# Two of six groups of a first matrix product in a second pass, five of eight blocks with seven products for eight

## The chip, the cores and the metric

The kernel runs on one core of a Trainium2 chip. The metric is device time in microseconds: the time of one execution, as a median over several runs. A profile of one execution is read beside it; its times are counted from the first instruction of its span.

The engines are named as in the profile: PE is TensorE (matrix products), PEld its loading of weights, DVE is VectorE, ACT is ScalarE, POOL is GpSimd, and SP is the engine that only issues DMAs here. Each engine takes its instructions in order.

## The reference

A block of linear attention with decay feeds a mixer. Everything is float32.

```python
# attention: batch 4, 8 heads, 768 positions, head size 64; blocks of 64 positions
intra = ((qb @ kb.T) * Dmask) @ vb
out[block] = intra + (qb * lam_pow) @ kv_state
kv_state = lam_block * kv_state + (kb * rev_pow).T @ vb

# mixer on x = attention output as (4, 768, 512)
h = x.transpose(0, 2, 1) @ U @ V           # U: 768 x 32, V: 32 x 768
u = x + h.transpose(0, 2, 1)
ch = np.maximum(u @ w_ch1, 0.0) @ w_ch2    # w_ch1: 512 x 2048, w_ch2: 2048 x 512
return u + ch
```

The two products with w_ch1 and w_ch2 are the bulk: 3,072 rows of u, 512 columns, 2,048 columns of the hidden layer.

## The kernel before

**Numbers.** The weights and the vectors arrive as 64-bit words; VectorE and ScalarE turn them into float32 on the chip. A conversion of one tile (128 x 512) has five VectorE steps (L166, L155, L184, L192, L197) and two ScalarE steps between them that make the exponents (L173, L174); the tiles `sc` and `m` that it works in exist once. A float32 factor is then split into a high part, a low part and a third, and a product of two factors takes three matrix products in a reduced format: high x high and low x low parts that go into a bank `pz`, and third x third into a bank `pd`; the result is `(4096 + 1) * pz + 4096 * pd`. This is why each 128 x 128 tile of weights costs three instructions of 512 columns.

**Stages.** (1) Attention over 24 tiles of 128 positions, up to about 114 us. Every tile's result `x_nat` gets the low-rank mix added (L571 for the last batch), is transposed on TensorE (L604 for the last eight tiles) and split into `u_hl` and `u_d`, and is stored to memory as `u_d` for the end. (2) The first product: u has six groups `g` of 512 positions, w_ch1 has 16 tiles `ft` of 128 hidden columns. `hidden(ft, pair)` does two groups for one `ft`: 16 matrix products into two `pz`, 8 into two `pd`, a ScalarE scaling (L844), a VectorE sum (L853) and a store of r to memory. (3) The second product: for each group and each `ft`, r is fetched, made positive and split (L952 on ScalarE, L953 and L954 on VectorE), and multiplied with w_ch2's tile, 12 matrix products; at the end of a group u is added (L994, and L998 on GpSimd) and the result goes out.

**Order.** Up to the end of the first six units of the first product (`head`), every engine's order is written out by hand (`manual_schedule`). There the last eight tiles of attention are mixed and transposed between the products (`rest`, `at`), and the conversions stand as `side` steps after given units. Afterwards a scheduler orders the instructions. `body` is the loop over `ft` with three pairs each, with the conversion and splitting of w_ch1's next tile (`w1_steps`) and of w_ch2 (`w2_steps`) as side steps; `tail` runs the last three `ft` pair by pair, so that the groups' places `hl` and `d` come free for w_ch2, which `w2_back` loads from memory, already split.

**Banks.** Eight banks, four tags (a1, a2, b1, b2) of two. A unit takes two for `pz` and two for `pd`, and units alternate between a and b.

Of the kernel before, what the change touches and what calls it, by code (L numbers as in the profile page):

```python
# [18 lines left out]
def kernel(  # L19
# [61 lines left out]
    mix_ctx = ctx.enter_context(ExitStack())  # L81
    att_ctx = ctx.enter_context(ExitStack())
# [19 lines left out]
    w2_d = [dram.tile([P, 3, C], FP32, name=f"w2_d{ft}") for ft in range(FT)]  # L102
# [100 lines left out]
    def split_steps(tile_of, src, in_parts=False, scale=None, apart=False):  # L203

        st = {}

        def dst():
            if "w" not in st:
                st["w"] = wconv.tile([P, C], FP32, tag="wf", name="wf")
            return st["w"]  # L210

        def five():
            st["o"] = o = tile_of()
            st["t"] = o[:, 0, :].bitcast(FP32)
            on_scalar(lambda: nc.scalar.mul(o[:, 0, :], st["w"], NEAR))  # L215

        def six():
            w, low = st["w"], st["o"][:, 1, :]
            st["low"] = low.bitcast(FP32) if scale is None else w
            nc.vector.tensor_tensor(  # L220
                out=low if scale is None else w, in0=w, in1=st["t"], op=ALU.subtract
            )
            if scale is not None:
                on_scalar(lambda: nc.scalar.mul(low, w, scale))

        def seven():
            nc.vector.scalar_tensor_tensor(
                st["o"][:, 2, :], st["t"], -E, st["low"], ALU.mult, ALU.add
            )

        return weight_steps(dst, src, C, in_parts=in_parts, apart=apart) + [five, six, seven]

    w1v, w2v = {}, {}

    def w1_steps(ft, in_parts=False, apart=False):
        def tile_of():
            w1v[ft] = w1_pool.tile([P, 3, C], F32R, tag="w1", name="w1")
            return w1v[ft]

        cols = moe_w_ch1[:, ft * P : (ft + 1) * P].rearrange("(c p) f -> p c f", p=P)  # L240
        return split_steps(tile_of, cols, in_parts, apart=apart)
# [340 lines left out]
    def columns(what, g, ct):  # L582
        return what[:, ct, :] if g >= FG else by_halves(what)[:, :, ct, :]

    def like(out, g):
        return out if g >= FG else out.rearrange("p (t i) -> p t i", i=D)

    hl_at, d_at = [hl_pool], [d_pool]
# [4 lines left out]
    def turn(s):  # L593

        g, n = divmod(s, TG)
        if n == 0:
            uhl[g] = hl_at[g >= FG].tile([P, 2, CT, N], F32R, tag="hl", name="u_hl")
            ud[g] = d_at[g >= FG].tile([P, CT, N], F32R, tag="d", name="u_d")
        if g >= FG:
            cols = slice(n * P, (n + 1) * P)  # L600
            hi, low, diff = uhl[g][:, 0, :, cols], uhl[g][:, 1, :, cols], ud[g][:, :, cols]
            pt = bank([P, CT, P], "put", "b1")
            for ct in range(CT):
                nc.tensor.transpose(  # L604
                    out=pt[:, ct, :], in_=xs[s][:, ct * P : (ct + 1) * P], identity=ident
                )
            store(s)
            del xs[s]
            nc.scalar.mul(hi, pt, E * NEAR)
            nc.vector.scalar_tensor_tensor(  # L610
                low, hi.bitcast(FP32), -1.0 / E, pt, ALU.mult, ALU.add
            )
            nc.gpsimd.tensor_tensor(
                out=diff, in0=hi.bitcast(FP32), in1=low.bitcast(FP32), op=ALU.subtract
            )
            return
# [187 lines left out]
    def enter_first_product(s):  # L804
        nonlocal r_pool
        att_ctx.close()
        words_pool[:] = [wconv]
        for pools, name in ((hl_at, "hl_b"), (d_at, "d_b")):
            pools.append(
                ctx.enter_context(tc.tile_pool(name=name, bufs=NG - FG, reuse_waits="tile"))  # L810
            )
        r_pool = ctx.enter_context(tc.tile_pool(name="r", bufs=4, reuse_waits="tile"))
        set_ends(r_pool.tile([P, 2], FP32, tag="ends", bufs=1, name="ends"))
# [9 lines left out]
    def hidden(ft, pair, before={}):  # L823
# [9 lines left out]
        for ct in range(CT):  # L833
            for n in range(2):
                for g in pair:
                    others()
                    nc.tensor.matmul(  # L837
                        out=like(acc[g][0], g), lhsT=w[:, n, ct, :],
                        rhs=columns(uhl[g][:, n], g, ct),
                        start=(ct == 0 and n == 0), stop=(ct == CT - 1 and n == 1),  # L840
                    )
# [3 lines left out]
        for ct in range(CT):  # L845
            for g in pair:
                others()
                nc.tensor.matmul(  # L848
                    out=like(acc[g][1], g), lhsT=w[:, 2, ct, :], rhs=columns(ud[g], g, ct),
                    start=(ct == 0), stop=(ct == CT - 1),  # L850
                )
# [4 lines left out]
    def w2_steps(ft):  # L856
        def tile_of():
            w2v[ft] = w2_pool.tile([P, 3, C], F32R, tag="w2", name="w2")
            return w2v[ft]

        def keep():
            nc.sync.dma_start(out=w2_d[ft], in_=w2v.pop(ft).bitcast(FP32))

        rows = moe_w_ch2[ft * P : (ft + 1) * P, :]
        return split_steps(tile_of, rows, scale=4096.0) + [keep]


    w2hl, w2dd = {}, {}

    def w2_back(ft):  # L870
        n, i = divmod(ft, 4)
        if i == 0:
            w2hl[n] = hl_pool.tile([P, 4, 2, C], F32R, tag="hl", name="w2_hl")
            w2dd[n] = d_pool.tile([P, 4, C], F32R, tag="d", name="w2_d")
        nc.sync.dma_start(out=w2hl[n][:, i].bitcast(FP32), in_=w2_d[ft][:, 0:2, :])
        nc.sync.dma_start(out=w2dd[n][:, i].bitcast(FP32), in_=w2_d[ft][:, 2, :])

    pairs = [(g, g + 1) for g in range(0, NG, 2)]

    LAST = FT - 3  # L880
    body = [(pair, ft) for ft in range(2, LAST) for pair in pairs]
    tail = [(pair, ft) for pair in pairs for ft in range(LAST, FT)]

    def run_units(units, side, every=lambda i: None):
        for i, (pair, ft) in enumerate(units):
            hidden(ft, pair)
            for step in side[len(side) * i // len(units) : len(side) * (i + 1) // len(units)]:
                step()
            every(i)

# [15 lines left out]
    head = [(pair, ft) for two in (pairs[:2], pairs[2:]) for ft in (0, 1) for pair in two]  # L906
    side = list(zip((0,), last[4:])) + list(zip((0, 3, 3, 3, 4, 4, 4, 4), w1_steps(2)))
    for i, (pair, ft) in enumerate(head):
# [10 lines left out]
    w2_pool = mid_ctx.enter_context(  # L919
        tc.tile_pool(name="w2v", bufs=2, side="right", reuse_waits="tile")  # L920
    )
# [3 lines left out]
    side = []  # L925
    for ft in range(3, FT - 1):
        side += w1_steps(ft) + w2_steps(ft - 3)
    side += w2_steps(FT - 4)
    run_units(body, side)
    side = w1_steps(FT - 1)  # L930
    for ft in range(LAST, FT):
        side += w2_steps(ft)
    backs = list(range(FT))
    run_units(tail[:6], side, lambda i: w2_back(backs.pop(0)) if i >= 2 else None)
    mid_ctx.close()


    m_pool = ctx.enter_context(tc.tile_pool(name="m", bufs=4, side="right", reuse_waits="tile"))
# [19 lines left out]
    spare = next(turns)  # L958

    def product(i, n, parts=range(3)):  # L960
        g, ft = steps[i]
        m, hl, dd = ms[i], w2hl[ft // 4][:, ft % 4], w2dd[ft // 4][:, ft % 4]
        if ft == 0:
            acc[n] = banks(1, n // 2 != spare)[0]
        pz, pd = acc[n]
        cols = slice(n * P, (n + 1) * P)
        first, end = ft == 0, ft == FT - 1
        if 0 in parts:
            nc.tensor.matmul(out=pz, lhsT=m[:, 0, cols], rhs=hl[:, 0], start=first, stop=False)  # L969
        if 1 in parts:  # L970
            nc.tensor.matmul(out=pz, lhsT=m[:, 1, cols], rhs=hl[:, 1], start=False, stop=end)  # L971
        if 2 in parts:
            nc.tensor.matmul(out=pd, lhsT=m[:, 2, cols], rhs=dd, start=first, stop=end)  # L973
# [9 lines left out]
    def finish(g, n, parts=[slice(0, C)]):  # L983
# [3 lines left out]
        if g == NG - 1:  # L987
            nc.vector.scalar_tensor_tensor(o, pz, 1.0 + E, u, ALU.mult, ALU.add)
        else:
            nc.scalar.mul(o, pz, 1.0 + E)  # L990
# [18 lines left out]
    for i, (pair, ft) in enumerate(tail[6:]):  # L1009
        hidden(ft, pair)  # L1010
        if i < 2:
            for n in range(2):
                w2_back(backs.pop(0))
        if i == 0:
            for n in range(3):
                fetch(n)
        if i == 1:
            for n in range(2):
                split(n)

    STAG = 3
    for i in range(len(steps) - STAG):
        g, ft = steps[i]
        ahead(i)
        if backs:
            w2_back(backs.pop(0))
# [46 lines left out]
```

## Time and profile before

| | us |
|---|---|
| median of 3 runs | 650.1 |
| lowest, highest | 649.54, 650.6 |
| span of the profiled execution | 648.1 |
| TensorE busy in it | 639.3 |
| VectorE busy | 434.7 |
| ScalarE busy | 268.8 |
| GpSimd busy | 116.3 |
| first product: first unit starts | 114.39 |
| second product: first matrix product starts | 382.88 |
| DMA, mean rate | 203 GB/s |

The profiled execution's own time is not given apart from its span; the span runs from the first to the last instruction, and the median of the timed runs is 2.0 us longer than this span. A span on PE is a model of when a matrix product ends, and one starts before the one ahead has ended, so the pace is read from the starts. The clock of TensorE was granted in full in all of the span.

### The profile page before, as it was taken

The numbers are of one execution on the slowest core, as the hardware profiler recorded it, in microseconds if no ns is written. First come the engines' busy times: TensorE is split into PE (matmuls) and PEld (weight loads), VectorE is DVE, ScalarE is ACT, GpSimd is POOL, SyncE is SP. The second block draws the span as 40 slices with busy tenths as digits, with TensorE's granted clock in tenths as the row PEclk, the third lists the DMA queues.
The fourth block names the chain that finished last, engine by engine and source line by source line (L and its number), as shares of the span: only waits on it lengthen the run. The fifth ranks groups of instructions, "written<-read, shape, count | busy, mean of one in ns | idle before, by whom it ended". The sixth has DMA issues, their size and how long they took to land.

```text
span 648.1 us, 13405 instructions
## 1 busy us (share of the span) xinstructions
PE 639.3 (99%) x5242; PEld 539.3 (83%) x5242; DVE 434.7 (67%) x709; ACT 268.8 (41%) x500; POOL 116.3 (18%) x104
## 2 busy tenths in 40 slices
PE   9899999999999999999999999999999999999997
PEld 8888989788888888888888888888888888888886
DVE  6656878668997777777796244685575665755854
ACT  3675766435755444444454222332322322322320
POOL 4475968330000000000000000030030300300300
PEclk9999999999999999999999999999999999999999
DMA  9979996354876555655587899864363363543521
GB/s 232 241 182 272 231 242 163 119 191 176 287 258 219 209 207 209 207 209 211 211 292 276 320 332 392 287 220 138 96 227 98 123 204 97 172 152 99 179 82 65
DMA packets 132737, 131.69 MB, mean 203 GB/s; under 512 B 81538, under 2 KB 90754, under 8 KB 132674
## 3 DMA queue, kind: packets, MB, share of 16 engines
q1 hardware_dynamic: 107552, 124.41, 59.1%
q10 hardware_dynamic: 25122, 6.42, 4.4%
q8 instruction: 41, 0.67, 0.4%
q14 instruction: 22, 0.18, 0.1%
HBM read 80.09 MB, written 50.33 MB: 201 GB/s over the span
## 4 chain that ended last, share of the span: by engine, by line
PE 97%; ACT 1%; issue 1%; DMA 1%; DVE 0%; ACTq 0%; DVEq 0%
PE pz L837 27%; PE pd L848 13%; PE pz L971 13%; PE pz L969 13%; PE pd L973 13%; PE px L459 4%; PE pss L408 4%; PE px L470 2%; PE pqk L361 2%; PE pkv L431 1%; PE pm L563 1%; PE pp L486 1%; PE pm L626 1%; DMA kraw<-in_k_dram 1%; PE put L604 1%
## 5 line engine op out<-in xcount | busy, mean ns | idle before, releaser
L837 PE MATMUL pz<-u_hl,w 128*128 128x512 f32 x768 | 185.0, 391 | 0.0
L837 PEld LDWEIGHTS pz<-u_hl,w 128*128 128x128 f32 x768 | 143.7, 188 | 30.2 <-ACT r L844 0.6
L971 PE MATMUL pz<-w_hl,m 128*128 128x512 f32 x384 | 148.7, 389 | 0.0
L969 PE MATMUL pz<-w_hl,m 128*128 128x512 f32 x384 | 148.3, 389 | 0.0
L973 PE MATMUL pd<-w_d,m 128*128 128x512 f32 x384 | 147.4, 389 | 0.0
L952 ACT ACTIVATE m<-rm 128x512 fp32r<-128x512 f32 x96 | 60.6, 632 | 182.3 <-PE pd L973 125.5
L953 DVE SCALAR_TENSOR_TENSOR m<-rm,m 128x512 fp32r<-128x512 f32 x96 | 71.6, 748 | 95.7 <-ACT m L952 95.7
L998 POOL TENSOR_TENSOR o<-o,u 128x512 f32<-128x512 f32 x20 | 29.8, 1523 | 433.1 <-DVE o L994 433.1
L853 DVE SCALAR_TENSOR_TENSOR r<-pd,r 128x512 f32<-128x512 f32 x96 | 61.7, 685 | 60.4 <-ACT r L844 48.2
L848 PE MATMUL pd<-u_d,w 128*128 128x512 f32 x384 | 95.7, 390 | 0.0
L971 PEld LDWEIGHTS pz<-w_hl,m 128*128 128x128 f32 x384 | 72.1, 188 | 15.0
L969 PEld LDWEIGHTS pz<-w_hl,m 128*128 128x128 f32 x384 | 72.1, 188 | 15.0
L973 PEld LDWEIGHTS pd<-w_d,m 128*128 128x128 f32 x384 | 72.1, 188 | 14.7
L848 PEld LDWEIGHTS pd<-u_d,w 128*128 128x128 f32 x384 | 72.0, 188 | 14.9
L844 ACT ACTIVATE r<-pz 128x512 f32<-128x512 f32 x96 | 51.7, 591 | 66.9 <-PE pz L837 66.9
L954 DVE SCALAR_TENSOR_TENSOR m<-m 128x512 fp32r<-128x512 f32 x96 | 74.7, 779 | 3.0
L417 DVE TENSOR_TENSOR sm<-pss,mask 128x512 f32<-128x512 f32 x48 | 30.9, 686 | 18.0 <-PE pss L408 17.8
L215 ACT ACTIVATE w<-wf 128x512 fp32r<-128x512 f32 x32 | 20.3, 633 | 36.5 <-DVE wf L197 28.7
L173 ACT ACTIVATE sc<-sc,ends 128x512 f32<-128x512 uint32 x30 | 21.6, 721 | 22.8 <-DVE sc L166 22.8
L459 PE MATMUL px<-vraw,sm 128*64 128x64 f32 x768 | 29.0, 228 | 1.6 <-issue 1.4
L408 PE MATMUL pss<-qt,kt 64*128 64x128 f32 x384 | 29.0, 290 | 0.6 <-issue 0.5
L459 PEld LDWEIGHTS px<-vraw,sm 128*64 128x64 f32 x768 | 25.9, 140 | 3.4 <-issue 2.5
(91 smaller groups left out, 606.6 us busy)
## 6 DMA issues: line engine op xcount, KB each, us to landing
r_d<-r SPq DMA_DIRECT2D x96, 256.0 KB, 2.5
rm<-r_d SPq DMA_DIRECT2D x96, 256.0 KB, 2.7
words<-in_moe_w_ch_dram SPq DMA_DIRECT2D x30, 512.0 KB, 4.2
w_d<-w SPq DMA_DIRECT2D x16, 768.0 KB, 3.4
w_hl<-w_d SPq DMA_DIRECT2D x16, 512.0 KB, 6.2
u_d<-x_nat SPq DMA_DIRECT2D x24, 256.0 KB, 4.4
u<-u_d SPq DMA_DIRECT2D x24, 256.0 KB, 4.5
qraw<-in_q_dram SPq DMA_DIRECT2D x23, 256.0 KB, 4.8
```

The costliest lines, as they stand in the source:

```text
L408: nc.tensor.matmul(out=pss[:, x, a, :], lhsT=kt[half[x], a, :], rhs=qt[half[x], a, :], start=True, stop=True,)
L459: nc.tensor.matmul(out=px[half[t], x, a, :], lhsT=sm[:, x, a, half[t]], rhs=vr[:, 2 * a + x, :], start=(a == 0), stop=(alone and a == HP - 1),
L837: nc.tensor.matmul(out=like(acc[g][0], g), lhsT=w[:, n, ct, :], rhs=columns(uhl[g][:, n], g, ct), start=(ct == 0 and n == 0), stop=(ct == ...
L844: nc.scalar.mul(rs[g], acc[g][0], 4096.0 + 1.0)
L848: nc.tensor.matmul(out=like(acc[g][1], g), lhsT=w[:, 2, ct, :], rhs=columns(ud[g], g, ct), start=(ct == 0), stop=(ct == CT - 1),)
L853: nc.vector.scalar_tensor_tensor(rs[g], acc[g][1], 4096.0, rs[g], ALU.mult, ALU.add)
L952: nc.scalar.activation(out=m[:, 0], in_=r, func=AF.Relu, scale=NEAR)
L953: nc.vector.scalar_tensor_tensor(m[:, 1], r, 0.0, hi, ALU.max, ALU.subtract)
L954: nc.vector.scalar_tensor_tensor(m[:, 2], hi, E, low, ALU.mult, ALU.subtract)
L969: nc.tensor.matmul(out=pz, lhsT=m[:, 0, cols], rhs=hl[:, 0], start=first, stop=False)
L971: nc.tensor.matmul(out=pz, lhsT=m[:, 1, cols], rhs=hl[:, 1], start=False, stop=end)
L973: nc.tensor.matmul(out=pd, lhsT=m[:, 2, cols], rhs=dd, start=first, stop=end)
```

## The change

The first pass now does groups 0 to 3 only, one group at a time (`single`); groups 4 and 5 (`g0`, `g1`) come after it, in a second pass over eight blocks `j` of two `ft` each.

- **Sums in one bank.** `single` accumulates the high and low products into one bank, ScalarE multiplies the bank in place by `1 + 2**-12` (`raise_high`), TensorE adds the thirds onto it two units later (`open_ends`), and ScalarE copies the bank to SBUF times 4096 (`to_memory`). VectorE has no part in it. `next_bank` goes through all eight banks.
- **Head.** Four units for six; w1(2) is converted after the second unit and split after the third. Groups 4 and 5 are kept unsplit (`whole`): after the transpose one ScalarE copy instead of three steps on three engines.
- **Five blocks with seven products for eight.** In the blocks `SEVEN` = 0, 2, 3, 5, 6 a 2 x 2 block product (two groups by two halves of the 512 columns, times two halves by two `ft`) is done by Strassen's method in Winograd's form: seven half products of six matrix products (`seven_of`), so 42 for the 48 of `eight_of`. The sums of u's parts (s1 to s4) are formed in the first pass's last units on VectorE and split (`form`), the sums of the weights' parts (`form_steps`) on VectorE right after conversion.
- **Weights of the second pass** are stored unsplit as forms (`forms_d`) and come back as 24 tiles of two forms, split by ScalarE (high), VectorE (low) and GpSimd (third) in `divided_steps`; w1 tiles have five buffers for three.
- **Chain of sums.** In `seven_of` a bank `z` goes on collecting (product 0, then 5, then 6, then 7), with a bank `d` for its thirds; ScalarE copies `z` into a bank `one_two` after product 0 so that product 1 can be added there; VectorE adds the pieces (`add_to`).
- **w_ch2** is stored unsplit (`w2_d`, 256 KB a tile) and split with `divided_steps` (third on VectorE) in blocks 4 to 7 and during the second product's first steps.

```diff
-    w2_d = [dram.tile([P, 3, C], FP32, name=f"w2_d{ft}") for ft in range(FT)]
+    w2_d = [dram.tile([P, C], FP32, name=f"w2_d{ft}") for ft in range(FT)]
+    forms_d = [dram.tile([P, 8, C // 2], FP32, name=f"forms_d{j}") for j in range(FT // 2)]
...
+    def divided_steps(parts, fetch, engine):
...
+        def split():
+            hi, low, third = parts()
+            w = st["w"][:, 0 : hi.shape[-1]]
+            nc.scalar.mul(hi, w, E * NEAR)
+            nc.vector.scalar_tensor_tensor(
+                low, hi.bitcast(FP32), -1.0 / E, w, ALU.mult, ALU.add
+            )
+            engine.tensor_tensor(
+                out=third, in0=low.bitcast(FP32), in1=hi.bitcast(FP32), op=ALU.subtract
+            )
...
-            nc.scalar.mul(hi, pt, E * NEAR)
-            nc.vector.scalar_tensor_tensor(
-                low, hi.bitcast(FP32), -1.0 / E, pt, ALU.mult, ALU.add
-            )
-            nc.gpsimd.tensor_tensor(
-                out=diff, in0=hi.bitcast(FP32), in1=low.bitcast(FP32), op=ALU.subtract
-            )
+            nc.scalar.copy(whole[g][:, :, n * P : (n + 1) * P], pt)
...
+    side = list(zip((0,), last[4:])) + list(zip((0, 1, 1, 1, 1, 2, 2, 2), w1_steps(2)))
...
+    HC = C // 2
+    SEVEN = (0, 2, 3, 5, 6)
+    LAST = FT - 4
...
+    def raise_high(acc):
+        nc.scalar.mul(acc, acc, 1.0 + E)
+
+    def to_memory(acc, ft, g):
+        r = r_pool.tile([P, N], FP32, tag="r", name="r")
+        nc.scalar.mul(r, acc, 4096.0)
+        nc.sync.dma_start(out=r_d[ft][g], in_=r)
...
+    def run_units(units, side):
+        for i, unit in enumerate(units):
+            open_ends.append(single(*unit))
+            if len(open_ends) > 2:
+                open_ends.pop(0)()
...
+    run_units([(g, ft) for ft in range(2, LAST) for g in range(FG)], side)
...
+    def seven_of(j, ends):
...
+        add_up(z, high_pieces((j, 0), "a11"), True)
...
+        one_two = next_bank("c11", rest)
+        nc.scalar.copy(one_two, z)
+        add_up(d, third_pieces((j, 0), "a11"), True)
+        c11 = taken(d, 4096.0)
...
+        add_up(five, high_pieces((j, 4), "s1"), True)
+        raise_high(five)
...
+        add_up(one_two, high_pieces((j, 1), "a12"), False)
+        raise_high(one_two)
...
+        on_chain(5, "s2")
+        c12 = both(z, d)
...
+        add_up(three, high_pieces((j, 3), "s4"), True)
+        raise_high(three)
+        add_up(five, third_pieces((j, 4), "s1"), False)
+        add_up(one_two, third_pieces((j, 1), "a12"), False)
+        add_to(c11, one_two)
+        give(c11, f, g0)
...
+        on_chain(6, "s3")
+        c22 = both(z, d)
+        add_to(c12, five)
...
+        add_up(three, third_pieces((j, 3), "s4"), False)
+        add_to(c12, three)
+        give(c12, f2, g0)
+        add_to(c22, five)
+        give(c22, f2, g1)
...
+        def end():
+            on_chain(7, "a22")
+            give(both(z, d), f, g1)
```

`both(z, d)` takes `z` times 4097 on ScalarE (`taken`) and adds `d` times 4096 on VectorE. The matrix products of the new parts all stand in `add_up`, one line.

## The prediction

> **What bounds the kernel now.** I read the page's busy times and slices first, then the chain, then TensorE in order of time.
>
> ```profile
> span 648.1 us, 13405 instructions
> ...
> PE 639.3 (99%) x5242; PEld 539.3 (83%) x5242; DVE 434.7 (67%) x709; ACT 268.8 (41%) x500; POOL 116.3 (18%) x104
> ...
> PEclk9999999999999999999999999999999999999999
> ...
> PE 97%; ACT 1%; issue 1%; DMA 1%; DVE 0%; ACTq 0%; DVEq 0%
> ```
>
> TensorE is busy for 99% of the span, at full clock, and 97% of the chain is TensorE. A busy PE need not be a fast one, so the pace comes from the timeline:
>
> ```profile
> 143.52 3.79 PE L837 MATMUL pz<-u_hl,w 128*128 128x512 f32 x16
> 147.15 1.98 PE L848 MATMUL pd<-u_d,w 128*128 128x512 f32 x8
> 148.96 3.79 PE L837 MATMUL pz<-u_hl,w 128*128 128x512 f32 x16
> ```
>
> A unit of 24 products starts every 5.44 us: 0.2267 us each. The first product's last unit starts at 377.44 and the second product at 382.88, again 5.44, and the view of waits names nothing TensorE waited for from 114 to 648. So each product removed is worth 0.2267 us, each wait added costs its whole length, and nothing but fewer products can gain.
>
> **What is removed.** In the order of the built program the first product has 1,122 matmuls of 512 columns for 1,152: the four first groups keep 4 x 16 x 12 = 768, the second pass has 5 x 42 + 3 x 48 = 354. 30 x 0.2267 = **6.8 us**. Products that accumulate in one bank one after another cost no more: in the last steps six on pz run at 0.227 (636.07 to 637.20). A reached semaphore costs nothing either: old units wait four times per 5.44 us at this same pace, and the new have about as many.
>
> **Where TensorE could now wait, in order of time.**
>
> *Head.* The conversion of w1(2) moves from the fourth unit to the second, and its five VectorE steps stand in the fixed order ahead of the fourth addition to x_nat (L571), which a transpose (L604) needs.
>
> ```profile
> 130.01 1.29 DVE L853 SCALAR_TENSOR_TENSOR r<-pd,r 128x512 f32<-128x512 f32 x2
> 131.22 0.68 DVE L571 TENSOR_TENSOR x_nat<-pu,x_nat 128x512 f32<-128x512 f32 x1
> ```
>
> On TensorE the transpose that reads this x_nat stands here:
>
> ```profile
> 134.84 0.60 PE L604 MATMUL put<-ident,x_nat 128*128 128x128 f32 x4
> ```
>
> Now at 131.22 the conversion starts. From the lines below, its first step to its fourth takes 1.96 us and the fourth step 0.72, plus 0.1 for ScalarE: the addition starts near 134.6 and ends near 135.3, and the transpose, due at 134.84, is 0.5 late, with all of TensorE's queue behind it. Bounds: 0 (the fifth step overlaps) to 1.2 (ScalarE takes a copy first). **0.5.**
>
> *First pass, single units.* A unit (12 products, 2.72 us) accumulates both parts in one bank; ScalarE scales the bank between them and copies it afterwards. No row has ScalarE writing PSUM; the neighbours are 591 ns (L844, PSUM to SBUF) and 632 (L952, SBUF), so I take 0.55 in a row (two of L844 last 1.09). The third part comes 5.44 us after the high part ends, because two other units lie between: 4.9 us of cover for the scaling. VectorE loses L853 here (0.685 each). But ScalarE now has two such steps per unit in its queue, mixed with the two exponent steps of each weight conversion:
>
> ```profile
> 144.76 0.42 DVE L166 TENSOR_SCALAR sc<-words 128x512 uint32<-128x512 uint32 x1
> 145.09 0.42 DVE L155 TENSOR_SCALAR m<-words 128x512 uint32<-128x512 uint32 x1
> 145.55 0.69 DVE L184 SCALAR_TENSOR_TENSOR m<-words,m 128x512 f32<-128x512 uint32 x1
> 146.72 0.69 DVE L192 SCALAR_TENSOR_TENSOR sc<-words,sc 128x512 uint32<-128x512 uint32 x1 [0.48 <-ACT sc L174]
> ```
>
> VectorE, ScalarE twice, VectorE: 1.96 from L166 to L192, then 0.72 and 0.72, so 3.4 us bare, and one buffer each for sc and m makes conversions follow one another. In the new order 18 of them (the fifth to the twenty-third) lie within 27 units, 27 x 2.72 = 73.5 us: 4.08 each. Walking ScalarE's and VectorE's rows in that order (0.55 per ScalarE step caught inside a conversion, 0.6 per VectorE step of a w1 split, 0.34 per 256-wide form) gives 4.3 on average: 18 x 0.22 = 4.0 us of drift against 4.9 of cover. A scaling queued behind the exponents is just about due. **0.7**, between 0 and the second rival.
>
> *Start of the second pass.* Count from the end of group 3's last high part. TensorE has 23 products (12 thirds of open units, 4 for z, 2 for d, 4 for p5, 1 for p3: 5.2 us) until the first that adds onto the copied bank c11. ScalarE has ahead of that copy: a scaling, two 1,024-wide form steps (kt, L367, takes 378 ns for 256 and 592 for 512, so about 1.0 in a row), three copies of sums, a weight split: 0.15 for the signal + 4 x 0.55 + 2 x 1.0 + 0.57 = 4.9, copy done at 5.5, seen at 5.6: **0.4** (0 to 1). Behind the waiting TensorE lies its whole queue. Next is bank d, which VectorE must have added to c12 before the third part of product 6, due at 10.4. VectorE's queue ahead of that addition, undisturbed: s3's low at 1.75 (after its 1.0 us high on ScalarE), a weight's low, s3's third and a21's low, 1.13 + 0.6 + 1.13 + 1.13, end 5.75 (a 1,024-wide step by 256 and 512: 424 ns of L439, 685 of L853); the next weight's low, released by ScalarE at 6.6, ends 7.3, a21's third 8.45, another weight's low (ScalarE at 8.4) 9.1, the addition 9.7. But GpSimd now makes the weights' thirds in between, and this is what GpSimd did to VectorE before:
>
> ```profile
> 425.21 2.49 DVE L994 SCALAR_TENSOR_TENSOR o<-pd,o 128x512 f32<-128x512 f32 x4
> 427.62 1.44 DVE L954 SCALAR_TENSOR_TENSOR m<-m 128x512 fp32r<-128x512 f32 x1
> 428.98 1.78 DVE L953 SCALAR_TENSOR_TENSOR m<-rm,m 128x512 fp32r<-128x512 f32 x1
> ```
>
> ```profile
> 425.97 5.94 POOL L998 TENSOR_TENSOR o<-o,u 128x512 f32<-128x512 f32 x4 [282.77 <-DVE o L994]
> ```
>
> Steps with both inputs in SBUF take 1.44 to 1.78 instead of 0.69; those reading PSUM (L994) stay at 0.62. About two splits or forms are hit, 2 x 0.95: 9.7 + 1.9 = 11.6 against 10.4, **1.2** (0 to 2). The Trainium skill, "SBUF — State Buffer", section "Who interferes with whom", speaks against the change here: a VectorE instruction with two SBUF inputs and a GpSimd one that reads SBUF exclude each other for the whole instruction. The rows above agree in kind. By that rule each hit would cost a GpSimd instruction of 1.29 to 1.35 (L613, L633), the wait would be 1.9, and the time 0.7 us more than forecast.
>
> *Rest of the second pass.* 354 x 0.2267 = 80.3 us. ScalarE has 64 steps at 0.59 and 24 weight splits at 0.63, 53 us; VectorE 35 sums at 0.685 and 24 splits at 0.69 to 1.78, 41 to 67, and 16 w2 splits; GpSimd 24 at 1.3 to 1.5, 36. Between a sum's end and the next product onto its bank lie 8 products for z (1.8 us for a 0.6 step) and 12 for d (2.7 for 0.6 + 0.7). **0**; the third rival if not.
>
> *Change to the second product.* Its first banks are the last blocks'; ScalarE copies them behind a w2 split: **0.3** (0 to 0.7). w2 is now stored whole (256 KB for 768) and split in blocks 4 to 7 and the second product's first steps, ScalarE 0.63 and VectorE 1.4, four steps (10.9 us) ahead of use; VectorE has there 1.4 per 2.72 for m. 0; uncovered, 0.7 per late tile. The DMA share (0.5 to 0.99 around 160 to 400) loses 16.8 MB of w2 and gains 13.0 MB of forms: 0. Groups 4 and 5 lose their splits in the head (8 x L609, L610, L613), hidden before: 0.
>
> **Sum.** 648.1 - 6.8 + 0.5 + 0.7 + 0.4 + 1.2 + 0.3 = 644.4 span. Times exceed spans by the launch: the median 650.1 is 2.0 over this span. So **646.4**. From no change this measurement tells about 0.2%, 1.3 us: 648.8 to 651.4 counts as same.
>
> **Rivals.** *Clean:* the order covers all waits; 643.3 to 644.6. For it: 67% VectorE, 41% ScalarE. Against: the head's transpose. Chance 0.13. *The conversion chain becomes the bound of the first pass* (slower): old conversions came every 5.2 to 5.4 us (L166 at 170.57, 175.76, 180.89, 186.09), with VectorE full but with L853 (1.2 us) among them. At 4.6 us each, 18 x 0.52 - 4.9 = 4.5 instead of 0.7, and with 0.5 + 0.4 + 1.2 + 0.3 all waits come to 6.9, the break-even; beyond it every 0.1 us costs 1.8: at 4.9 the waits are 12.3 and the time 655.6. For it: the bare chain leaves no more than 0.7 for ScalarE's inserted steps; against: removing L853 frees more than they cost. 0.16. *The stream of weights comes late in the second pass:* a tile serves 12 products (2.7 us), is held up to 7.3 us, and five buffers leave 13.6 - 7.3 = 6.3 us for refilling it; split and third take 0.63 + 1.78 + 1.5 = 3.9 at worst, but loads queue on SP behind stores that wait for VectorE. If each of five blocks loses 1 us: 651.4; with less, 649. 0.13. *The products are not saved:* excluded by the count but for 0.02.
>
> **How the numbers follow.** My own case, 644.6 to 648.6, has 0.56. Faster: 0.56 + 0.13, less a little at the edge, 0.68; same: the third rival, 0.13; slower: the second and what is left, 0.19. The range 643.4 to 652.5 leaves out the edge of the clean case and the upper part of the second rival.
>
> **What would show it.** After the change: the pace of 0.2267 kept; in the waits, TensorE on VectorE's x_nat once (0.5), on ScalarE's scaling pz after some 75 us of single units (0.7), on c11's copy (0.4) and on r<-d (1.2) at the start of the second pass; GpSimd near 36 us busy there and weight splits of over 1 us. A sum of waits above 6.8, or gaps at each block, makes it wrong.

## The result and the profile after

| | before | after |
|---|---|---|
| median, us | 650.2 (4 runs, 649.54 to 650.6) | 657.3 (4 runs, 655.22 to 658.13) |
| ratio of the times, 95% interval | 1 | 1.0109 (1.009 to 1.0128) |
| span of the profiled execution | 648.1 | 656.2 |
| second product starts | 382.88 | 390.09 |

Slower by 1.1%, where 646.4 was forecast. From the page of the changed kernel:

```profile
span 656.2 us, 13585 instructions
...
PE 637.8 (97%) x5212; PEld 532.3 (81%) x5212; DVE 455.7 (69%) x714; ACT 327.1 (50%) x604; POOL 139.7 (21%) x120
...
PEclk9999999999999999999999999999999999999999
...
PE 77%; DMA 8%; DVE 6%; ACT 5%; issue 3%; ACTq 0%; DVEq 0%; SPq 0%
```

The 30 matrix products are gone (5,212 instructions for 5,242), at full clock. But the chain that ended last is TensorE for 77% only, 97% before; a DMA has come into it with 8%. The view of waits says what TensorE waited for from 114 us on (in total, times, longest); before, this view was empty:

```profile
PE pz L934 <- ACT pz L941: 7.8, 8, 1.7
PE d L934 <- DVE r L1118: 1.1, 1, 1.1
PE p L934 <- ACT p L941: 0.6, 1, 0.6
PE pz L1245 <- ACT r L945: 0.5, 1, 0.5
PE put L639 <- DVE x_nat L606: 0.4, 1, 0.4
```

Of the five places that the prediction priced, `x_nat`, `d` and the change to the second product (L1245) are there, the first two at about their size. The copy of c11 has no line here, and the wait on `p` was not forecast. The scaling of `pz` in the first pass is eleven times its size. The named times are idle times. What a wait costs is read from the starts of the products, in the timeline:

```profile
149.80 1.07 PE L934 MATMUL pz<-u_d,w 128*128 128x512 f32 x4
...
228.14 1.98 PE L934 MATMUL pz<-u_hl,w 128*128 128x512 f32 x8
231.33 1.19 PE L934 MATMUL pz<-u_d,w 128*128 128x512 f32 x4 [1.21 <-ACT pz L941]
232.36 1.99 PE L934 MATMUL pz<-u_hl,w 128*128 128x512 f32 x8
...
304.50 1.98 PE L934 MATMUL pz<-u_d,w 128*128 128x512 f32 x8
```

Eight products from 228.14 end at 229.95, so the thirds at 231.33 are 1.38 late for 1.21 named, and these four take 1.03 for 0.91. Unit 0's thirds start at 149.80 and unit 53's at 304.50. 634 products start in between (53 units of 12, less two that unit 3 has done before 149.80): 154.7 us for 634 x 0.2267 = 143.7. **The first pass lost 11.0 us**, 10.0 of them at the eight waits. The expectations below have 10.5 for it, from twelve products in every unit. How such a wait comes about, all engines from the same view:

```profile
221.76 0.38 SPq L148 DMA_DIRECT2D words<-in_moe_w_ch_dram  x1
...
228.85 0.43 DVE L168 TENSOR_SCALAR sc<-words 128x512 uint32<-128x512 uint32 x1 [1.14 <-DMA words<-in_moe_w_ch_dram]
...
229.31 0.72 ACT L175 ACTIVATE sc<-sc,ends 128x512 f32<-128x512 uint32 x1 [2.05 <-DVE sc L168]
...
230.07 0.72 ACT L176 ACTIVATE sc<-sc,ends 128x512 uint32<-128x512 f32 x1
230.70 0.58 ACT L941 ACTIVATE pz<-pz 128x512 f32<-128x512 f32 x1
```

Read it backwards from 231.33. The scaling TensorE waited for began at 230.70, behind two exponent steps of a conversion. ScalarE had been idle for 2.05 us at the first of them, because VectorE had not begun that conversion; VectorE was idle for 1.14 us, because the words had not landed. Their load was issued at 221.76, the moment the conversion two ahead had read the same buffer (L194, 221.04 to 221.73), and took 7.0 us. For all conversions of the first pass, the view of the tile `words` has:

```profile
  DMA words<-in_moe_w_ch_dram: 14.5, 10
  ACT sc L176: 11.1, 18
...
DMA to landing us min/median/max: 3.6/5.0/7.0
```

VectorE waited ten times, 14.5 us, for words; a load took 5.0 us (before the change 4.2, and VectorE never began a conversion late for it). From the eighth to the 25th conversion, counted from that of w1(2), the words lay ready for 0.5 us on average before VectorE took them; before the change it was 0.9 us or more for every load whose landing is recorded. SP was mostly not what delayed the issue: the load stood first in its queue, waiting for L194, 16 times of 28, for 23.7 us.

### The profile page after: what moved, and what is told of

Same layout as the page of the kernel before. It is cut to its first block, busy times and chain, and to the rows that moved or that the text cites. A ratio compares the mean times of both kernels' runs of the same rounds, so it can differ in the third digit from the quotient of the medians.

```text
span 656.2 us, 13585 instructions
## 1 busy us (share of the span) xinstructions
PE 637.8 (97%) x5212; PEld 532.3 (81%) x5212; DVE 455.7 (69%) x714; ACT 327.1 (50%) x604; POOL 139.7 (21%) x120
## 4 chain that ended last, share of the span: by engine, by line
PE 77%; DMA 8%; DVE 6%; ACT 5%; issue 3%; ACTq 0%; DVEq 0%; SPq 0%
PE pz L1245 13%; PE pz L1247 13%; PE pd L1249 13%; PE pz L934 13%; DMA words<-in_moe_w_ch_dram 6%; PE px L494 4%; PE pss L443 4%; PE z L934 2%; PE pz L869 2%; PE px L505 2%; PE p L934 2%; PE pqk L396 2%; DVE sc L194 2%; PE pkv L466 1%; ACT sc L176 1%
## 5 line engine op out<-in xcount | busy, mean ns | idle before, releaser
L1245 PE MATMUL pz<-w_hl,m 128*128 128x512 f32 x288 | 112.0, 389 | 0.0
L1247 PE MATMUL pz<-w_hl,m 128*128 128x512 f32 x288 | 112.0, 389 | 0.0
L1249 PE MATMUL pd<-w_d,m 128*128 128x512 f32 x288 | 110.7, 389 | 0.0
L934 PE MATMUL pz<-u_hl,w 128*128 128x512 f32 x448 | 110.7, 389 | 0.0
L934 PEld LDWEIGHTS pz<-u_hl,w 128*128 128x128 f32 x448 | 84.1, 188 | 17.8
L934 PE MATMUL pz<-u_d,w 128*128 128x512 f32 x224 | 61.2, 395 | 7.8 <-ACT pz L941 7.8
L1247 PEld LDWEIGHTS pz<-w_hl,m 128*128 128x128 f32 x288 | 54.1, 188 | 11.3
L1249 PEld LDWEIGHTS pd<-w_d,m 128*128 128x128 f32 x288 | 54.1, 188 | 11.2
L1245 PEld LDWEIGHTS pz<-w_hl,m 128*128 128x128 f32 x288 | 54.1, 188 | 11.2
L934 PEld LDWEIGHTS pz<-u_d,w 128*128 128x128 f32 x224 | 41.2, 188 | 20.2 <-ACT pz L941 12.1
L941 ACT ACTIVATE pz<-pz 128x512 f32<-128x512 f32 x68 | 39.6, 583 | 16.7 <-PE pz L934 16.7
L1245 PE MATMUL pz<-w,m 128*128 128x512 f32 x96 | 37.5, 390 | 0.5 <-ACT r L945 0.5
L1247 PE MATMUL pz<-w,m 128*128 128x512 f32 x96 | 37.4, 389 | 0.0
L1249 PE MATMUL pd<-w,m 128*128 128x512 f32 x96 | 37.3, 390 | 0.0
```

Of the source, the lines that this page charges most:

```text
L934: nc.tensor.matmul(out=out, lhsT=weights, rhs=moving, start=start and i == 0, stop=i == len(pieces) - 1, skip_group_check=not start,)
L941: nc.scalar.mul(acc, acc, 1.0 + E)
L1245: nc.tensor.matmul(out=pz, lhsT=m[:, 0, cols], rhs=hi, start=first, stop=False)
L1247: nc.tensor.matmul(out=pz, lhsT=m[:, 1, cols], rhs=low, start=False, stop=end)
L1249: nc.tensor.matmul(out=pd, lhsT=m[:, 2, cols], rhs=third, start=first, stop=end)
```

## The experiments

The runs below shared their runs of the kernel before, which spread more there (649 to 656.6) than above, so ratios are given. In profiles the attention stage ended some 5 us apart for nearly the same code, so stages are compared from the transpose of the fourth `x_nat` (135.20 in the changed kernel's profile) to the second product's first matrix product: 254.9 us after the change, 248.0 before it (134.84 to 382.88).

Theory A is the round trip of the words: with two buffers, 5 us for a load, some 3 us to the end of the conversion's last reading step, and 1 us on average between them and on SP make some 9 us for two conversions. Theory B is the prediction's second rival: ScalarE's scalings and copies, mixed with the exponent steps, make the chain of conversions too long by themselves.

**A third buffer for the words** (`words_three`).

```diff
-        return wconv.tile([P, C], FP32, tag="tmp", bufs=2, name=name)
+        return wconv.tile([P, P], FP32, tag="tmp", bufs=2, name=name)
...
+    words_pool.append(mid_ctx.enter_context(
+        tc.tile_pool(name="words2", bufs=1, side="right", reuse_waits="tile")))
```

> A third buffer for the 64-bit words of a weight (the room comes from a temporary of attention whose tile was larger than what it used); nothing else is edited, the scheduler orders anew. Theory A, the round trip of the words: with two buffers a load can be issued only when the conversion two ahead has read its words (L194), it stands on SP behind a store of r, lands 5.0 us after its issue, and the conversion then needs 2.0 to 2.8 us to its own L194: some 9.2 us for two conversions, 4.6 each, for the 4.08 that TensorE's pace allows. Then a third buffer brings a conversion to at most 4.2 us, VectorE's waits for words (14.5 us) fall under 3, TensorE's waits for the scaling in the first pass (7.8 us, 10.5 with the slow restarts) under 2, and the time is near 648. Theory B, the mixing on ScalarE: the exponent steps stand behind scalings and copies that wait for TensorE, whatever the words do. Then conversions still take 4.5 us and the time is 655 to 657.

Ratio to the kernel before 0.9972 (0.9947 to 0.9998). Its waits, TensorE's and VectorE's:

```profile
PE pz L934 <- ACT pz L941: 0.8, 1, 0.8
...
DVE sc L194 <- ACT sc L176: 11.2, 19, 0.9
...
DVE sc L168 <- DMA words<-in_moe_w_ch_dram: 4.2, 3, 2.0
```

One wait of 0.8 for eight of 7.8, and the stage takes 245.8 us, 9.1 less. The seventh to the 25th conversion start at 176.42 and 248.50, 4.00 us each; in the changed kernel at 175.04 and 257.25, 4.57 each. Loads were no quicker (5.4 us), only earlier: the words now lay ready for 3.2 us on average. VectorE's waits for words fell to 4.2 us and not under 3. VectorE's wait for ScalarE within a conversion is the same 11 us, so B's mechanism exists, but with the words in time the chain fits into TensorE's 4.08. Theory A. It does not rest on this order alone: the four later kernels with a third buffer, in five profiles, have at most one wait for a scaling in the first pass, of 0.29 (three of the four also add the thirds a unit later).

**Thirds four units later** (`lag_four`): does more cover do it too?

```diff
-            if len(open_ends) > 2:
+            if len(open_ends) > 4:
```

> A unit's thirds are added four units later and not two, so that a scaling has 10.3 us of cover for 4.9. Both theories: the conversions keep their pace of about 4.6 us, a drift of 18 x 0.5 = 9 us is now covered, TensorE's waits for the scaling fall from 7.8 us to under 2 and the time is 647 to 650. If instead the drift is not bounded by the first pass (the weights themselves are late), TensorE waits for the weight tiles and the time stays at 654 or more.

Ratio 1.0013 (0.9991 to 1.0035): as fast as before the change, less than expected. The pace of conversions stayed (175.43 to 257.05, 4.53 each) and TensorE no longer waited for a scaling in the first pass (once, 0.6 us, for a copy that frees a bank), so that the drift is the conversions' own and not made by TensorE's waits. But the crowd at the second pass's start was later on VectorE, and this came of it (waits; then the busy times by stretch, where the third column from the right is the granted clock):

```profile
PE d L934 <- DVE r L1118: 2.3, 1, 2.3
```

```profile
308.00:309.00 1.00, 0.70 (x2) 0.64 (x3) 0.90 (x3) 0.86 (x2) 0.98 (x1) 0.70 0.36 99
309.00:310.00 1.00, 1.00 (x3) 0.75 (x3) 1.00 (x2) 0.32 (x1) 0.00 (x0) 0.50 0.93 210
310.00:311.00 1.00, 1.00 (x4) 0.76 (x3) 1.00 (x3) 0.44 (x1) 0.77 (x1) 0.50 0.78 285
311.00:312.00 1.00, 1.00 (x4) 0.79 (x3) 1.00 (x3) 0.20 (x1) 0.52 (x1) 0.59 0.96 265
312.00:313.00 1.00, 1.00 (x6) 0.81 (x5) 1.00 (x2) 0.03 (x1) 0.31 (x1) 1.00 0.92 292
```

After an idle time of 2.3 us TensorE had half its clock for 3.4 us (0.6 + 1 + 1 + 0.8), and by the starts of the products 1.7 us were lost on top.

**The first pass with two banks** (`two_banks`), VectorE adding the thirds as before the change.

```diff
-        raise_high(acc)
+        r = taken(acc, 4096.0 + 1.0)
...
-            add_up(like(acc), [...], False)
-            to_memory(acc, ft, g)
+            pd = next_bank("pd")
+            add_up(like(pd), [...], True)
+            add_to(r, pd), give(r, ft, g)
```

> The first pass as it was before the change in one respect: thirds in a bank of their own, ScalarE scales the first bank into SBUF once, VectorE adds the second; one group at a time, the rest as changed. Theory B: ScalarE has one step less per unit, TensorE waits for no scaling; but VectorE gets 0.685 us per 2.72, so a conversion (3.0 us of VectorE, splits and forms about 0.8 more) comes near 4.9 us and the weight tiles come late instead: 652 to 658, with TensorE waiting for w and not for pz. Theory A: the loads still bound at 4.6 or more, and the wait shows on the weight tiles as well: 653 to 660. If the in-place scaling itself were the trouble, not the conversions: 648 or less.

Ratio 1.006 (1.0029 to 1.0091). Neither theory's place was right: the weights came in time, and TensorE waited for nothing in the first pass. VectorE was the bound (busy for 145 of the 150 us from 150 to 300, for 118 in the changed kernel; its waits for words from 140 to 300 fell to 1.6 us), its conversions went on to 324.5 instead of 285.4, and the backlog was paid on the bank `d`:

```profile
PE d L934 <- DVE r L966: 3.3, 2, 3.1
```

again with half the clock for 3.4 us behind the 3.1. So it takes two things to lose 11.0 us in the first pass: late conversions, and sums in one bank, which let TensorE wait for ScalarE's queue.

**All blocks with eight products** (`all_eight`): is a product saved worth its 0.2267 us? The second edit adds the first pass's open thirds in a block of eight, which `seven_of` did.

```diff
-    SEVEN = (0, 2, 3, 5, 6)
+    SEVEN = ()
...
             raise_high(acc)
+            while open_ends:
+                open_ends.pop(0)()
```

> All eight blocks with eight products: 30 products more, 6.8 us; the waits at the second pass's start on the bank d (1.4 with the restart), on c11 (0.3) and on p (0.6) gone, and with the forms of the weights' sums 20 VectorE steps of 0.34 us gone from the first pass. If each product saved is worth 0.2267 us and the first pass's waits stay as they are: 657.3 + 6.8 - 2.3 = 661.8; with up to 3 us less waiting in the first pass 659. If the seven-product blocks cost what they save: 657 or less.

Ratio 1.019 (1.0148 to 1.0231), 662.6 beside 650.2. Its stage takes 260.0 us, 5.1 more than the changed kernel's, with waits of 8.3 us there

```profile
PE pz L934 <- ACT pz L941: 8.3, 10, 1.8
```

for 9.5 in the changed kernel and 0.12 lost at c11: 5.1 + 1.2 + 0.1 = 6.4, for the forecast 6.8. The saving is real. The first pass has nine of these waits, 7.9 us, without the sums of the weights' parts: those VectorE steps are not what made the conversions late.

**The thirds of the stream on VectorE** (`thirds_on_vector`).

```diff
-        stream_steps.append(divided_steps(parts, fetch, nc.gpsimd))
+        stream_steps.append(divided_steps(parts, fetch, nc.vector))
```

> The changed kernel with one edit: the thirds of the second pass's weights are made by VectorE and not by GpSimd. If the slow steps of VectorE at the start of the second pass (L1066 at 2.23 us for 1.2, L263 at 1.78 for 0.68) come from GpSimd's thirds running beside them, all its 512-wide steps there take 0.68 to 0.69 and the 1,024-wide ones 1.2, and the wait on bank d (1.1 us) falls to between 0 and 0.9, since at most three thirds (0.6 each) now stand ahead of the addition. If GpSimd has no part in it, the long steps stay and the wait grows by up to 2 us. The first pass is as it was (8 waits, 7.8 us), so the time is 655 to 657 either way.

654.5 us in one run. The wait on `d` was gone, and the view of L263 says why (durations min, median, max; first the changed kernel, then this one):

```profile
L263 DVE SCALAR_TENSOR_TENSOR w<-w,wf x28: 425/684/1827, 271.5 to 380.2; 128x512 fp32r<-128x512 f32 x27, 128x256 fp32r<-128x256 f32 x1
```

```profile
L263 DVE SCALAR_TENSOR_TENSOR w<-w,wf x28: 416/684/693, 271.4 to 376.5; 128x512 fp32r<-128x512 f32 x27, 128x256 fp32r<-128x256 f32 x1
```

No step was slow without GpSimd beside it; L1066 fell from a longest of 2.23 us to 1.23. The slowing is GpSimd's. The wait on p went as well, one of 0.9 came on the last block's bank, and the first pass kept its waits (5.4 us in 7).

**a21 split after the first sum** (`a21_late`, a single run, and `a21_late_timed`), with the third words buffer.

```diff
-    for step in form("s3", 3, 0, s3) + form("a21", 3, 1, a21):
+    for step in form("s3", 3, 0, s3):
         step()
...
+    a21_steps = form("a21", 3, 1, a21)
...
+            if j == 0 and i == 4:
+                for step in a21_steps:
+                    step()
```

> On top of the third buffer for words: a21 is split after block 0's second sum and not before the first (it is first needed in block 1). ScalarE loses one 1,024-wide step (1.05 us) ahead of the copy of c11, VectorE two (1.2 each) ahead of the addition on bank d. If the wait on d is what the prediction said (VectorE's queue ahead of the addition), TensorE waits for neither: 1.1 and 0.3 us with 0.3 to restart, 1.4 to 1.7 in all less than with the third buffer alone. If another step comes last there (the copy of z by ScalarE, the weights' splits), a wait of over 0.5 stays.

> The version with only the third buffer for words and the late split of a21, timed: its single profile had no wait in the first pass and none at the second pass's start, with 0.59, 0.24 and 0.51 us at p and at the second product. From the fifth transpose of the last batch to the end it took 509.9 us, for 513.3 before the change and 508.8 for the last mended version. If these profiles are typical: 0.9950 of the kernel before, and 1 us over the mended version. If the first pass's freedom from waits was chance (the third buffer alone had one wait of 0.77): 0.997.

In the first profile no wait was left up to the second pass's block 6, neither on `d` nor on c11: both were queues ahead of them, as the prediction had it. Timed, 0.9925 (0.99 to 0.995), better than the 0.9950 expected; the second profile had one wait of 0.29 in the first pass.

**Every named wait at once** (`all_mended`, `all_mended_w2`, `mended_no_pool`). Besides the third buffer (and the one that is free first is used first) and the late a21:

```diff
-            if len(open_ends) > 2:
+            if len(open_ends) > 3:
...
-            rest.append((unit, i - 3, "mix", c0 + n + 1))
+            rest.append((*((1, 22) if n == 2 else (unit, i - 3)), "mix", c0 + n + 1))
...
-    spare = 1
+    spare = 0
```

> Third buffer for words (the buffer that is free first comes first), thirds three units later and not two, a21 split late, the fourth addition to x_nat ahead of the conversion of w1(2), and the second product starting on banks that no sum of the second pass holds. Each edit is meant to take one wait away that the traces name. With the third buffer alone, 245.8 us lay between the transpose that reads the fourth x_nat and the second product, for 248.0 before the change; less the waits on d (1.4 with the restart), x_nat (0.7), the weights' split (0.5) and the scaling (1.1): 242.1, and 0.8 off behind it, so 5.9 + 0.8 under the kernel before, less 0.9 for a wait on p that stays: 644 to 645.5 beside 650.2. Rival: the waits move instead of going (with thirds four units later the wait on d rose from 1.1 to 2.3 us): 647 to 649.

> The same, with w_ch2's tiles fetched and split one block later (from block 5, and three steps ahead in the second product). The wait on p in block 6 (0.7) stood behind a split of w_ch2 on ScalarE that waited 1.3 us for its load: if the load is late because of the crowd of stores and loads on SP, one block later does not help and the wait moves to the start of the second product (0.5 to 1.0 slower than the other); if it is only the place in ScalarE's queue, 0.7 to 1.0 faster.

0.9956 (0.9932 to 0.998) and 0.9944 (0.9927 to 0.9962), which is 647.3 and 646.6 beside 650.2. The first is a miss (644 to 645.5 expected; 647 to 649 was the rival, that waits move): with `spare = 0` the wait at the second product's start was 1.3 us and not gone; it had moved to a bank whose copy stood on ScalarE behind a split of w_ch2 that waited 2.5 us for its load. With w_ch2 one block later (from block 5) it was gone, but p's stayed (0.7), as did one of 0.45 behind a split of m that waited 3.1 us for its load. The two ratios' intervals overlap, so the gain of 0.7 us is not shown. The last version is this one with the thirds on VectorE:

> The last version (all mended, w_ch2 one block later) with the second pass's thirds on VectorE. Its profile had waits on the first block of eight (0.45), p (0.70) and d (0.18), each with 0.3 to restart, 2.2 us in all. If the wait on d is what is left of GpSimd's slowing of VectorE, it goes (0.5); the other two stand behind ScalarE steps that wait for a load (a split of m on r's load for 3.1 us, a split of w_ch2 on its own for 1.3), so they stay unless the scheduler's new order moves those steps. VectorE has 24 x 0.685 = 16 us more in 80 us of which it is idle for 18 or more. 0.5 to 1.5 us faster than the last version: 0.992 to 0.994 of the kernel before. Rival: VectorE becomes the bound of the second pass, and the time is 1 to 3 us longer than the last version's.

0.9919 (0.9891 to 0.9948), the lowest ratio of all, though a21 late alone lies within its interval. Its waits from 114 us on:

```profile
PE pz L934 <- ACT pz L941: 0.6, 1, 0.6
PE put L639 <- DVE x_nat L606: 0.6, 1, 0.6
PE c L934 <- ACT c L1148: 0.3, 1, 0.3
```

In this order the second product's first matrix product (377.66) stands ahead of the last four of the second pass, which end their turn at 379.73. From the same transpose (135.86) the stage's own products take 379.73 - 0.23 - 135.86 = 243.6 us for 248.0 before: 4.4 of the 6.8 us are there, and these three waits with their restarts account for the rest.

## Why the prediction was wrong

- **Removed: right.** 6.8 us forecast, 6.4 by `all_eight`. The pace of 0.2267 held wherever nothing waited.
- **Head: right.** 0.5 forecast; the transpose started at 135.20 where its place was 134.64, 0.56 late. With the addition ahead of the conversion (`all_mended`) this wait is gone.
- **First pass, single units: the step that failed, 0.7 forecast, 11.0 measured.** "Walking ScalarE's and VectorE's rows in that order ... gives 4.3 on average" counted engines and left out the load. SP's L148 can only be issued when a buffer of words is free, and there are two; before the change, conversions came every 5.2 us at the closest and hid a load of 4.2, and nothing was left of that at 4.08 with 5.0. Measured 4.57. With the words in time it is 4.00, less than the walk's 4.3. The cover was too large as well: at the seventh conversion a scaling (176.12) began 2.3 us after TensorE had gone on from its high part (173.83), so of "4.9 of cover" 2.6 were left. Nine conversions, from 175.04 to 214.41, drifted by 39.37 - 9 x 4.08 = 2.6 us, and the first wait came at 216.13. Nor did the drift end with the 18 conversions that were counted: 5.2 of the 11.0 us were lost behind the 25th, as the next five took 28.1 us (21.0 with the third buffer).
- **The rival that came true** is the second, with the chance 0.16, by another cause. It put 655.6 at 4.9 us each. At the measured 4.57 its own sum gives 18 x 0.49 - 4.9 = 3.9 us for the first pass, not 11.0, for the cover of 4.9 was not there and the drift went on. That 655.6 lies near the measured 657.3 is luck.
- **Start of the second pass: right.** c11, 0.4 forecast (0 to 1): the copy ended at 309.66, 5.2 us after the last high part and not 5.5, and the first product onto c11 started in its place, 309.71, though its load of weights had waited 0.26 for the copy; the nine products from 308.58 to 310.74 lost 0.12. Bank `d`, 1.2 forecast, 1.28 late (315.88 for 313.69 + 4 x 0.2267), 1.36 with the slow restart. VectorE's steps ahead of the addition are those that the prediction lists, and it ended 11.2 us after the last high part, for 11.6 forecast. Two hits by GpSimd of about 0.95 each were forecast; the timeline has two, 1.0 and 1.1 (between them stand the lines of c11):

```profile
308.18 1.29 POOL L266 TENSOR_TENSOR w<-w 128x512 fp32r<-128x512 f32 x1 [1.98 <-DVE w L263]
308.32 2.23 DVE L1066 SCALAR_TENSOR_TENSOR s_d<-s_hl 128x1024 fp32r<-128x1024 f32 x1 [0.22 <-PE pz L934]
...
309.71 0.76 PEld L934 LDWEIGHTS c<-s_hl,w 128*128 128x128 f32 x4 [0.26 <-ACT c L1147]
309.71 1.19 PE L934 MATMUL c<-s_hl,w 128*128 128x512 f32 x4
...
312.21 1.21 DVE L1066 SCALAR_TENSOR_TENSOR s_d<-s_hl 128x1024 fp32r<-128x1024 f32 x1
312.43 2.16 POOL L266 TENSOR_TENSOR w<-w 128x512 fp32r<-128x512 f32 x1 [2.95 <-DVE w L263]
...
313.35 1.78 DVE L263 SCALAR_TENSOR_TENSOR w<-w,wf 128x512 fp32r<-128x512 f32 x1
```

  The step that comes second waits, on either engine: VectorE at 308.32, GpSimd at 312.43, VectorE again at 313.35. The Trainium skill, "SBUF — State Buffer", section "Who interferes with whom", has this as a rule, a lock for a whole instruction. The trace agrees; the rule's full price was not paid, since each waiter came after the other had begun.
- **Rest of the second pass: 0 forecast, 0.9.** Block 6's p was queued on ScalarE behind a split of w_ch2 whose load was late, which the sum had not costed:

```profile
376.02 0.63 ACT L262 ACTIVATE w<-wf 128x512 fp32r<-128x512 f32 x1 [1.53 <-DMA wf<-w_d]
376.56 0.58 ACT L941 ACTIVATE p<-p 128x512 f32<-128x512 f32 x1
```

- **Change to the second product: 0.3 forecast, 0.9** (391.81 for 391.00, and 0.1 to restart).

In all 0.56 + 11.0 + 0.12 + 1.36 + 0.9 + 0.9 = 14.8, of the 656.2 - 641.3 = 14.9 us by which the span exceeds the one without a wait. The prediction's other terms sum to 2.4 and measured 3.8; the one term made the difference of sign.

## What to carry to other kernels

A step that had slack had it on every resource: when its period is cut from 5.2 to 4.1 us, check each round trip through it, the refilling of its buffers too, at (load + use) / buffers, and not the engines' rows alone. The bare sum here, (5.0 + 3.0) / 2 = 4.0, fits into 4.08 with nothing to spare, and with loads of 3.6 to 7.0 us it came to 4.57. An engine that issues in order hands a late load on to whatever stands behind: here a matrix product waited for a DMA that it has nothing to do with, by way of two exponent steps on ScalarE. Four kilobytes of each partition for a third buffer, three of them from an oversized temporary, turned 1.1% slower into 0.3% faster.

## What the runs showed of the hardware

- Idle times of TensorE of up to 1.85 us (`all_eight`) in the first pass left the clock at full; 2.3 us (`lag_four`) and 3.1 us (`two_banks`) were each followed by 3.4 us at half clock, in `lag_four` from the moment the products resumed, in `two_banks` 1 us later. The Trainium skill, "TensorE: Matmul & The Clock Gate", section "HAM oscillation — how this bites in real kernels", warns of idle gaps above about 3.4 us; here 2.3 were enough. Length alone does not decide: a gap of 3.04 us in the attention stage of `all_eight` (24.53 to 27.57) cost no clock, one of 1.94 in that of `all_mended` (86.53 to 88.48) did. Every stretch between two changes of the clock was a multiple of 3.413 us (78.5 = 23 x, 297.0 = 87 x, 300.4 = 88 x). On that grid the three drops each end an interval with 1.94 to 2.31 us of idle time, while a border of `all_eight` at 26.22 (its clock rose to full at 9.16, and 5 x 3.413 later is 26.22) divides the 3.04 into 1.69 and 1.35. That idle time per interval decides is inferred from these four gaps, not tested.
- A short wait costs about 0.3 us more than the idle time that the profile names: 7.8 us named, 10.0 lost, in eight waits.
- ScalarE scales 128 x 512 in PSUM in place in 0.58 us and copies it to SBUF in 0.59; two in a row start 0.48 to 0.52 apart, near the 0.55 assumed.
